# A three-stage attention and MLP kernel: a new order of the middle stage with eight exponential buffers, stack loads ahead in their block, whole-chunk loads for the attention output, and ten instead of twelve warming matmuls

## The chip, the cores and the metric

The kernel runs on one core of one Trainium2 chip. The metric is the device time of one execution in microseconds. Before the change it is 696.94 us, the median of three runs (695.82 to 697.39). A core has a matrix engine (PE, with its weight loads PEld), a vector engine (DVE), an activation engine (ACT), a general engine (POOL) and a queue engine (SP) that issues most of the DMAs here. Each engine works through its own list in order; between engines and DMAs stand semaphores.

## The reference

The output mixes two branches per token, with a gate from the token itself:

```python
x = A_x                                                  # 1 x 2048 x 512
g = sigmoid((x * gate_w).sum(-1, keepdims=True))
qkv = x @ wqkv                                           # 32 heads of 16
scores = einsum("bhqd,bhkd->bhqk", q, k) * 16 ** -0.5
mask = (i - j >= 0) & (i - j < 256)                      # sliding causal window
a = (softmax(where(mask, scores, -1e9)) @ v) @ wo
y = (x - mean(x)) / sqrt(var(x) + 1e-5)
b = gelu(y @ w1 + b1) @ w2 + b2                          # 512 -> 1792 -> 512
out = g * a + (1 - g) * b
```

Everything is float32. The kernel splits each operand of a large matmul into a high and a low part and adds three products (high x high, low x high, high x low), so a 512-deep product takes twelve matmuls of 128 x 128 x 512.

## The kernel before

The program has three stages, and its tile framework is told not to reorder: the instructions of each engine stand in the order in which the Python code emits them.

**Stage 1** (to 145 us in the profile) projects x to q, k and v. It opens with `first_units`: a zeroed tile `idle` is multiplied with itself twelve times (L265) while the first weights and the first chunk of x arrive, then 24 matmuls (L281) make the first two q/k units. q and k go to DRAM in a layout from which "stacks" of four heads are loaded later.

**Stage 2** (145.3 to 494.5 us) interleaves attention and the first MLP layer on PE. The table `ORDER` is a string of 1202 letters, and `run` emits one piece of work for each:

- `S` (`s_pair`, L348): scores of one block of 128 queries, for the row maximum alone; read by DVE (L357, L358).
- `T` (`st_pair`, L403): the transposed scores of one block of keys, with the maximum in two extra rows; ACT exponentiates them (L405) and POOL zeroes what the mask forbids (L407). There are eight groups `p` of four heads, sixteen blocks `kb` each, and two `T` (pr 0 and 1) per block.
- `P` (`pv`, L422): 32 matmuls that multiply the exponentials of up to four key blocks with v, for two blocks of queries; ACT copies the result out.
- `f` (`fill`, L626): one step, two matmuls, of a unit of the first MLP layer; 24 steps make a unit, of which there are 28. ACT copies the unit's two halves to `t` tiles (`out_half`), and SP stores them to `hp`.

All four take their PSUM from four buffers of two banks, `ring`: the next piece takes the buffer that was used longest ago, and a unit of the MLP keeps one for its 24 steps. The exponentials of a key block live in one of seven slots taken in rotation (`p_tile`), three and two in two tiles and two in the spare `x8` tiles `extra`. There are nine `t` tiles, which hold the halves, raw weights and the collected outputs of `P` (`acc`).

At the start of each block `kb`, `block` first calls `tick()`, which emits what earlier pieces left for later (stores of `hp` and `osc`, weight swaps), and then, for even `kb`, the two DMAs of `load_stacks` (L335), which bring 256 columns of the next group's q and k; the `S` of the next group run about six blocks ahead of its `T`. The maxima go out and come back as DMAs (`md`, L376 and L382).

**Stage 3** (from 494.5 us) runs the second MLP layer in 56 steps of twelve matmuls (`mlp2`, L834; four chunks of 512 tokens with 14 steps each). Into each chunk go four attention output units of twelve matmuls (`attn_out`, L813), one per 128 tokens. In `attn_out(c)`, SP loads the softmax sums (`su`, L785), DVE inverts them two steps later (`inv`, L790), SP stores the inverse (`rd`, L791), and then for each 128 tokens `loads(b)` issues eight DMAs, four of the attention output `osc` (L797) and four of the repeated inverse (L798), 64 KB each, into two `t` tiles. `scale` (L801) multiplies them two steps after that, ACT and DVE split the product, and one step later come the matmuls. Stage 3 has 44 `t` tiles.

## Time and profile before

| what | value |
|---|---|
| median of three runs | 696.94 us (695.82 to 697.39) |
| the profiled execution | 699.85 us, of which 698.0 us from its first to its last instruction (the span) |
| granted TensorE clock, mean | 0.999 |
| busy: PE, PEld | 688.7 us (99%), 536.0 us (77%) |
| busy: DVE, ACT, POOL | 474.9 us (68%), 385.1 us (55%), 268.8 us (39%) |
| DMA | 137.93 MB, mean 198 GB/s |

A row of the profile names the source line, the engine, the operation and the tiles it writes and reads (out<-in), then the shape and the count; behind a bar stand busy time, mean duration and idle time. A row of the timeline gives the start, the length of a run of equal instructions, and in brackets the engine's idle time before it with what ended it. A matmul's record begins when it begins to stream and ends when its result is out, so the records of neighbours overlap, and the distance between two starts tells the pace, not the length of one. A small wait between two matmuls therefore does not show as idle time of PE.

### The profile page before, as it was taken

What the parts mean: (1) busy time and instruction counts of PE and PEld (TensorE: products, weight loads), DVE (VectorE), ACT (ScalarE), POOL (GpSimd) and SP (SyncE); (2) the same over time, 40 slices, a digit from 0 to 9 for tenths busy, and PEclk for the clock granted to TensorE, in tenths of its full rate; (3) what the DMA queues carried; (4) which work ended last, traced back from release to release, by engine and by line L of the source; (5) the groups of instructions that cost most, each with busy time, mean ns of one, the idle gap of its engine ahead of it and who ended that gap; (6) DMA issues with size and microseconds to landing.
All of it is one profiled execution on the core that took longest, in us unless ns stands there. A gap on an engine that the chain in (4) does not pass through costs nothing.

```text
span 698.0 us, 16035 instructions
## 1 busy us (share of the span) xinstructions
PE 688.7 (99%) x5740; PEld 536.0 (77%) x5740; DVE 474.9 (68%) x971; ACT 385.1 (55%) x639; POOL 268.8 (39%) x623
## 2 busy tenths in 40 slices
PE   9999999999999999999999999999999999999997
PEld 6887777877777767777787777777777788888886
DVE  6546779966868777777687786776456835645554
ACT  6447463457686775777767768677624414123121
POOL 6900156436476564755656656559000000000000
PEclk9999999999999999999999999999999999999999
DMA  8998888786565758647776656525856443543531
GB/s 311 363 319 259 251 253 261 231 258 192 181 217 171 218 171 262 187 147 231 204 218 190 200 163 186 165 92 191 282 167 186 146 142 116 169 139 111 183 108 60
DMA packets 102678, 137.93 MB, mean 198 GB/s; under 512 B 13928, under 2 KB 53800, under 8 KB 102472
## 3 DMA queue, kind: packets, MB, share of 16 engines
q1 hardware_dynamic: 97848, 128.66, 58.7%
q10 hardware_dynamic: 4752, 8.26, 3.6%
q8 instruction: 46, 0.75, 0.4%
q14 instruction: 32, 0.26, 0.1%
HBM read 81.53 MB, written 54.30 MB: 195 GB/s over the span
## 4 chain that ended last, share of the span: by engine, by line
PE 89%; SPq 3%; DMA 3%; DVE 1%; issue 1%; ACT 1%; POOL 1%; DVEq 0%; ACTq 0%
PE ps_b L626 21%; PE ps_a L834 17%; PE ps_d L294 12%; PE ps_b L422 12%; PE ps_b L403 7%; PE ps_b L348 7%; PE ps_d L324 6%; PE ps_o L813 5%; SPq L797 1%; SPq L798 1%; DMA b2s<-in_b 1%; PE ps_d L281 1%; PE ps_x L265 1%; DMA osc<-t 1%; PE ps_x L348 1%
## 5 line engine op out<-in xcount | busy, mean ns | idle before, releaser
L626 PE MATMUL ps_b<-x,w 64*128 64x512 f32 x1344 | 212.7, 396 | 0.3 <-ACT p L405 0.2
L407 POOL TENSOR_SCALAR_AFFINE_SELECT p<-p 128x256 f32<-128x256 f32 x344 | 133.3, 415 | 102.5 <-ACT p L405 99.6
L405 ACT ACTIVATE p<-ps_b 128x768 f32<-128x768 f32 (+2 forms) x184 | 137.9, 770 | 42.5 <-PE ps_b L403 32.1
L834 PE MATMUL ps_a<-x,t 128*128 128x512 f32 x648 | 150.6, 390 | 0.8 <-DVE t L686 0.8
L358 DVE TENSOR_REDUCE mx<-ps_b 128x2 f32<-128x512 f32 x208 | 144.1, 693 | 7.1
L834 PEld LDWEIGHTS ps_a<-x,t 128*128 128x128 f32 x648 | 121.4, 188 | 27.3 <-issue 1.2
L626 PEld LDWEIGHTS ps_b<-x,w 64*128 64x128 f32 x1344 | 129.2, 186 | 11.9 <-issue 2.9
L357 DVE COPY_PREDICATED ps_b<-tri,ps_b 128x256 f32<-128x256 uint8 x208 | 88.3, 425 | 50.1 <-PE ps_b L348 34.7
L403 PE MATMUL ps_b<-qk 50*128 50x384 f32 (+5 forms) x512 | 90.3, 344 | 0.5 <-DVE mx L358 0.3
L348 PE MATMUL ps_b<-qk 62*128 62x384 f32 (+3 forms) x472 | 85.2, 346 | 1.4 <-DMA qk<-qk 1.3
L294 PE MATMUL ps_d<-x,w 128*128 128x512 f32 x360 | 84.8, 391 | 0.0
L294 PEld LDWEIGHTS ps_d<-x,w 128*128 128x128 f32 x360 | 67.3, 188 | 14.5 <-issue 0.5
L422 PE MATMUL ps_b<-p,v 128*32 128x256 f32 (+1 forms) x1376 | 74.9, 329 | 0.4 <-POOL p L407 0.4
L122 ACT ACTIVATE t<-ps_b 128x512 f32<-128x512 f32 (+1 forms) x112 | 52.0, 490 | 40.0 <-PE ps_b L422 32.8
L403 PEld LDWEIGHTS ps_b<-qk 64*128 64x128 f32 (+1 forms) x512 | 50.9, 184 | 20.7 <-issue 6.5
L407 POOL TENSOR_SCALAR_AFFINE_SELECT x<-x 128x256 f32<-128x256 f32 x136 | 52.2, 410 | 35.4 <-ACT x L405 35.1
L405 ACT ACTIVATE x<-ps_b 128x768 f32<-128x768 f32 (+2 forms) x72 | 55.0, 778 | 16.4 <-PE ps_b L403 13.6
L348 PEld LDWEIGHTS ps_b<-qk 62*128 62x128 f32 (+1 forms) x472 | 46.3, 184 | 17.9 <-ACT p L405 4.0
L422 PEld LDWEIGHTS ps_b<-p,v 128*32 128x32 f32 x1376 | 39.1, 110 | 26.5 <-ACT p L405 3.5
L119 DVE TENSOR_TENSOR t<-t,t 128x512 fp32r<-128x512 f32 x70 | 48.5, 692 | 14.6 <-ACT t L122 10.9
L122 ACT ACTIVATE t<-t 128x512 fp32r<-128x512 f32 x16 | 10.1, 632 | 81.7 <-DVE t L801 37.0
L682 ACT ACTIVATE t<-t,b1s 128x512 f32<-128x512 f32 x56 | 37.8, 715 | 25.4 <-DMA t<-hp 24.9
(87 smaller groups left out, 672.4 us busy)
## 6 DMA issues: line engine op xcount, KB each, us to landing
qk<-qk SPq DMA_DIRECT2D x112, 196.0 KB
t<-hp SPq DMA_DIRECT2D x56, 256.0 KB
hp<-t SPq DMA_DIRECT2D x52, 256.0 KB
qk<-t SPq DMA_DIRECT2D x48, 256.0 KB
osc<-t SPq DMA_DIRECT2D x31, 256.0 KB
t<-in_w SPq DMA_DIRECT2D x28, 256.0 KB
w<-w SPq DMA_DIRECT2D x28, 256.0 KB
qk<-t ACTq DMA_DIRECT2D x24, 256.0 KB
```

The source lines that it names most:

```text
L119: eng.tensor_tensor(out=lo, in0=src, in1=f32(hi), op=ALU.subtract)
L122: act.activation(dst, src, AF.Copy)
L294: pe.matmul(o, a[:, dt * 128:(dt + 1) * 128], b[:, dt * C:(dt + 1) * C], start=n == 0, stop=n == 11)
L348: pe.matmul(o[:, e, :n], qs[pr][r:k, qb * 128:qb * 128 + 128], ks[pr][r:k, t0:t0 + n], start=True, stop=True)
L357: dve.copy_predicated(o[:, :, :128], tri, o[:, :, 256:384])
L358: dve.tensor_reduce(m, o[:, :, :256], mybir.AxisListType.X, ALU.max)
L403: pe.matmul(o[:, e, :w], ks[pr][r:k, kb * 128:kb * 128 + 128], qs[pr][r:k, kb * 128:kb * 128 + w], start=True, stop=True)
L405: act.activation(pt[:, :, :w], o[:, :, :w], AF.Exp, scale=0.25)
L407: pool.affine_select(out=pt[:, :, a:a + 128], in_=pt[:, :, a:a + 128], pattern=[[0, 2], [sgn, 128]], base=b, channel_multiplier=-sgn, comp ...
L422: pe.matmul(a[32 * h:32 * h + 32, at:at + w], vs[:, kb, v:v + 32], pts[p, kb][:, h, fr:fr + w], start=n == 0, stop=n == len(parts) - 1, sk ...
L626: pe.matmul(o[:, e], w[kt // 4][r:r + 64, k, m:m + 128], y[r:r + 64, a:a + C], start=n == 0, stop=n == 23)
L834: pe.matmul(accs[c][b], x[:, b * 128:(b + 1) * 128], w, start=f == 0 and n == 0, stop=f == FT - 1 and n == 2)
```

## The change

Five places change. The text of `ORDER` is new throughout (1204 letters), and so its rows say little; the first line of each stands in the diff.

```diff
-ORDER = ("TfSffSffffTSffffTSfffTfSffTfSfffTSfffSPTSTSffffTSfffTfSfPTSffSfffTSffTffTfSfTffffSTPSTSPSTfTfffTSfff"
+ORDER = ("TfSfSfffffTfSfffTSfffTfSfffTSfffTfSffSPTSffTfSfffTSfffSPSTfSfffTfSfTffTffTSffTfffTSPSSTPSTfTfffTSffT"
...
+PICK = ("0000000000000000001000000000000000000001000100100000000000000000100001000100000000000001000000000000"
...
-    ring = []
+    ring, picks = [], list(PICK)
+
+    def choose():
+        return ring.pop(int(picks.pop(0)) if picks else 0)
 
     def two():
         if not ring:
             return ps("x", (128, 2, 512))
-        ring.append(ring.pop(0))
+        ring.append(choose())
         return ps(ring[-1], (128, 2, 512))
...
-        dve.memset(idle, 0.0)
+        dve.memset(idle[:, :256], 0.0)
         idle = idle.bitcast(BF16)
         o = two()[:, 0]
-        for _ in range(12):
+        for _ in range(10):
             pe.matmul(o, idle[:, :128], idle[:, :512], start=True, stop=True)
...
         if j % 2 == 0:
-            acc[p] = t2()
+            sums.append(sums.pop(0))
+            acc[p] = sums[-1]
...
-    nt[0] = 9
+    nt[0] = 6
...
-    extra = [f32(x8())[:, :1536].rearrange("p (h n) -> p h n", h=4) for _ in range(2)]
+    extra = [f32(x8()) for _ in range(2)]
+    sums = [t[:, 1536:] for t in extra]
+    extra = [t[:, :1536].rearrange("p (h n) -> p h n", h=4) for t in extra]
...
-    slots = [get("work", "p3", 1, (128, 3, 4, 384)), get("work", "p2", 1, (128, 2, 4, 384))]
-    slots = [slots[0][:, 0], slots[0][:, 1], extra[0], slots[0][:, 2], slots[1][:, 0], extra[1], slots[1][:, 1]]
+    low, high = (get("work", t, 1, (128, 3, 4, 384)) for t in ("pa", "pb"))
+    slots = [low[:, 0], low[:, 1], extra[0], low[:, 2], high[:, 0], extra[1], high[:, 1], high[:, 2]]
 
     def p_tile():
         np_[0] += 1
-        return slots[(np_[0] - 1) % 7]
+        return slots[(np_[0] - 1) % 8]
...
     def mlp1_unit(f, cp):
-        held = ring.pop(0)
+        held = choose()
...
     def block(p, kb):
-        tick()
         if kb % 2 == 0:
             if kb and p + 1 < 8:
                 load_stacks(p + 1, kb * 128 - 256, 256)
             if not kb and p:
                 load_stacks(p, S - 256, 256)
+        tick()
...
-    nt[0] = 44
+    nt[0] = 36
...
+        o = get("work", "oa", 1, (128, 4, 512))
+
+        def load_o():
+            for g in range(NG):
+                sp.dma_start(o[:, g], view(osc, [32 * S, HG], [S, DH], [1, C], off=g * 256 * S + c * C))
+
+        if c:
+            load_o()
 
         def inv():
             dve.reciprocal(su, su)
             sp.dma_start(view(rd, [128, 128], [1, 128]), su)
             us[c] = get("work", "us", 2, (128, 4, 512))
-
-        def loads(b):
-            o, r = t2(F32, (128, 4, 128)), t2(F32, (128, 4, 128))
+            r = get("work", "ra", 1, (128, 4, 512))
+            if not c:
+                load_o()
             for g in range(NG):
-                sp.dma_start(o[:, g], view(osc, [32 * S, HG], [S, DH], [1, 128], off=g * 256 * S + c * C + b * 128))
-                sp.dma_start(r[:, g], view(rd, [C, HG], [0, DH], [1, 128], off=g * HG * C + b * 128))
-
-            def scale():
-                dve.tensor_tensor(out=o, in0=o, in1=r, op=ALU.mult)
-                h, l = t2(F32R, (128, 4, 128)), t2(F32R, (128, 4, 128))
-                copy(h, o)
-                lo_part(l, o, h)
-                after(1, lambda: mm(h, l))
...
+                sp.dma_start(r[:, g], view(rd, [C, HG], [0, DH], [1, C], off=g * HG * C))
+            for b in range(4):
+                after(3 + b, lambda b=b: scale(b, *(t[:, :, b * 128:b * 128 + 128] for t in (o, r))))
...
-            after(2, scale)
+            after(1, mm)
 
         after(2, inv)
-        for b in range(4):
-            after(3 + b, lambda b=b: loads(b))
```

`PICK` says for each piece which of the free PSUM buffers it takes (0 is the one used longest ago; 522 of its 583 entries are 0, 60 are 1, one is 2). The eighth exponential slot takes the memory of three `t` tiles, and the collected outputs of `P` move to the unused ends of the two `extra` tiles. In stage 3, `inv` now emits the loads of a whole chunk and asks for `scale(b)` three to six steps after itself, which is the step where it stood before, so that the order on PE there stays what it was; `oa` and `ra` take the memory of eight `t` tiles. Line numbers behind the first edits grow: L335 is now L344, L403 is L412, L422 is L431, L626 is L638, L797 is L804 and L798 is L817.

The change moves instructions at three places of which the prediction speaks. First SP's list in chunk 0 of stage 3, from the sums' loads on; `w` are raw weights, `hp` the stored first-layer halves. Before:

```order
L785 DMA su_7623<-osc 32x1x128 x4
L655 DMA t_7646<-in_w 128x512
L679 DMA t_7648<-hp 128x512
L791 DMA rd_7628<-su_7623 128x128
L655 DMA t_7670<-in_w 128x512
L679 DMA t_7672<-hp 128x512
L797 DMA t_7693<-osc 128x1x128
L798 DMA t_7694<-rd_7628 128x1x128
L797 DMA t_7693<-osc 128x1x128
L798 DMA t_7694<-rd_7628 128x1x128
```

and with the change:

```order
L797 DMA su_7589<-osc 32x1x128 x4
L667 DMA t_7613<-in_w 128x512
L691 DMA t_7615<-hp 128x512
L811 DMA rd_7594<-su_7589 128x128
L804 DMA oa_7595<-osc 128x1x512 x4
L817 DMA ra_7637<-rd_7594 128x1x512 x4
L667 DMA t_7646<-in_w 128x512
L691 DMA t_7648<-hp 128x512
L667 DMA t_7670<-in_w 128x512
L691 DMA t_7672<-hp 128x512
```

The four pairs for the first 128 tokens, and 24 more DMAs for the other three quarters behind them, become eight DMAs directly behind the store of the inverse, and the loads of step 11 stand behind these.

Second, SP's list in stage 2 around the stacks of group 3, columns 1024 to 1279 (`qk<-qk_1`, `qk<-qk_0`; the one of `qk_0_69` onto itself is a copy in DRAM). Before:

```order
L522 DMA w_3228<-w_3227 64x1024 x2
L639 DMA hp<-t_3441 128x512
L639 DMA hp<-t_3443 128x512
L435 DMA osc<-t_3470 128x512
L335 DMA qk_79<-qk_1_68 98x2x256
L335 DMA qk_79<-qk_0_67 98x2x256
L315 DMA qk_0_69<-qk_0_69 16x8x512
L376 DMA md_3452<-ms_3451 4x32x32
```

and with the change:

```order
L532 DMA w_3234<-w_3233 64x1024 x2
L651 DMA hp<-t_3430 128x512
L651 DMA hp<-t_3432 128x512
L344 DMA qk_79<-qk_1_68 98x2x256
L344 DMA qk_79<-qk_0_67 98x2x256
L445 DMA osc<-x_254_1522 128x512
L324 DMA qk_0_69<-qk_0_69 16x8x512
L385 DMA md_3441<-ms_3440 4x32x32
```

The stacks pass the store of `osc`.

Third, PE's list at the end of stage 2, around the last `P` but one (its four rows of matmuls into one PSUM tile). Before:

```order
L403 MATMUL ps_b_1122_7385<-qk_79 128x256 x2
L403 MATMUL ps_b_1123_7390<-qk_79 128x256 x2
L422 MATMUL ps_b_1124_7395<-p_256_1526,v_80 32x256 x4
L422 MATMUL ps_b_1124_7395<-p_255_1525,v_80 32x128 x4
L422 MATMUL ps_b_1124_7395<-x_254_1524,v_80 32x256 x4
L422 MATMUL ps_b_1124_7395<-p_256_1526,v_80 32x128 x4
L403 MATMUL ps_b_1126_7418<-qk_79 128x128 x2
L403 MATMUL ps_b_1127_7423<-qk_79 128x128 x2
```

and with the change:

```order
L412 MATMUL ps_b_1091_7352<-qk_79 128x256 x2
L412 MATMUL ps_b_1092_7357<-qk_79 128x256 x2
L638 MATMUL ps_b_1061_7140<-x_212_1256,w_5787 128x512 x2
L412 MATMUL ps_b_1095_7374<-qk_79 128x128 x2
L412 MATMUL ps_b_1096_7379<-qk_79 128x128 x2
L638 MATMUL ps_b_1097_7384<-x_193_1143,w_6234 128x512 x2
L431 MATMUL ps_b_1098_7387<-pa_1523,v_80 32x256 x4
L431 MATMUL ps_b_1098_7387<-x_253_1521,v_80 32x128 x4
L431 MATMUL ps_b_1098_7387<-pb_1524,v_80 32x256 x4
L431 MATMUL ps_b_1098_7387<-x_254_1522,v_80 32x128 x4
```

Two MLP steps and the last two `T` now stand ahead of this `P` instead of behind it.

36 lines of the change are left out of this document (23 added, 13 removed).

## The prediction

> **What bounds the kernel now.** I read the page first, then the waits of PE, then the busy time by stage.
>
> ```profile
> PE 688.7 (99%) x5740; PEld 536.0 (77%) x5740; DVE 474.9 (68%) x971; ACT 385.1 (55%) x639; POOL 268.8 (39%) x623
> PE ps_b L348 <- DMA qk<-qk: 1.3, 1, 1.3
> PE ps_a L834 <- DVE t L686: 0.8, 1, 0.8
> 145.30:494.50 349.20, 346.57 (x4249) 261.95 (x4248) 261.67 (x588) 250.45 (x384) 209.96 (x552) 1.00 0.62 193
> 494.50:545.30 50.80, 49.58 (x211) 38.64 (x210) 28.42 (x50) 21.98 (x37) 0.00 (x0) 1.00 0.60 188
> 545.30:694.00 148.70, 148.70 (x657) 122.90 (x655) 81.02 (x137) 39.68 (x62) 0.00 (x0) 1.00 0.41 131
> ```
>
> PE is busy for 99% of the span, and its waits view has two entries in stages 2 and 3 above 0.5 us. (The rows of stages give length, then PE, PEld, DVE, ACT, POOL, clock, DMA share, GB/s.) Read so, nothing but matmuls could be gained. But records of neighbours overlap, so the loss must be read from the distance between starts:
>
> ```profile
> 568.80 2.88 PE L813 MATMUL ps_o<-w,t 128*128 128x512 f32 x12
> 571.52 2.88 PE L834 MATMUL ps_a<-x,t 128*128 128x512 f32 x12
> 467.10 1.51 PE L422 MATMUL ps_b<-p,v 128*32 128x256 f32 x32
> 468.42 0.61 PE L422 MATMUL ps_b<-x,v 128*32 128x256 f32 x8
> 472.37 0.34 PE L403 MATMUL ps_b<-qk 64*128 64x384 f32 x2
> 472.55 0.40 PE L626 MATMUL ps_b<-x,w 64*128 64x512 f32 x2
> L626 PE MATMUL ps_b<-x,w 64*128 64x512 f32 x1344 | 212.7, 396 | 0.3 <-ACT p L405 0.2
> ```
>
> Twelve matmuls of 512 columns take 2.72 us at pace, 0.227 each; one `P` (32 records) 1.32; a full `T` or `S` up to 0.18 (472.37 to 472.55); an MLP step, two matmuls side by side, as long as one of 512 columns. Stage 2 holds 672 steps (1344 records), 256 `T` and 236 `S`, of which some are narrower, and 64 `P`, of which eight are half: 672 x 0.227 + 492 x 0.17 (less 5 for the narrow ones) + 60 x 1.32 = 152.5 + 78.6 + 79.2 = 310 us. It lasts 349.2. So some 39 us of stage 2 are lost in pieces too small for the waits view, and this is what a new order can win or lose. In stage 3 the same pace shows no loss from 545 us on (the groups from 568.80 stand 2.72 apart), and some in chunk 0.
>
> **The start: ten warming matmuls.**
>
> ```profile
> 0.98 0.48 DVE L261 MEMSET t<- 128x512 f32 x1 [0.98 <-PEq L874]
> 1.52 5.30 PE L265 MATMUL ps_x<-t 128*128 128x512 bf16 x12 [1.52 <-DVE t L261]
> 5.34 0.15 PEld L265 LDWEIGHTS <-t 128*128 128x128 bf16 x1 [0.28 <-issue]
> 5.76 0.15 PEld L265 LDWEIGHTS <-t 128*128 128x128 bf16 x1 [0.28 <-issue]
> 5.06 0.43 DVE L236 CAST x<-v 128x512 fp32r<-128x512 f32 x1 [3.59 <-DMA v<-in_xt]
> 5.23 0.51 ACT L122 ACTIVATE w<-wv 128x128 fp32r<-128x128 f32 x2 [1.73 <-DMA wv<-in_wq]
> 5.98 0.68 DVE L119 TENSOR_TENSOR x<-v,x 128x512 fp32r<-128x512 f32 x1
> 6.26 6.41 PE L281 MATMUL ps_d<-x,w 128*128 128x512 f32 x24
> 6.26:7.40 1.14, 1.14 (x2) 0.93 (x3) 1.00 1.05 404
> ```
>
> A warming matmul takes 0.427 us (their weight loads stand 0.42 to 0.43 apart), twice the later pace. The first real operands are there at 5.49 (x) and about 5.5 (w), but the last warming matmul starts at 6.19 and holds PE to 6.61; by 7.40 only two real matmuls have begun (the last row), also at 0.43. With ten, and with a memset of half the columns (0.24 us less), the warming ends at 1.28 + 10 x 0.427 = 5.55. PE has 1.06 us more for real matmuls. If the clock rises at the same moment, 2.5 of them run in that time at half speed, worth 2.5 x 0.227 = 0.57 us. The next operand, the low part of x, is there at 6.66 and needed at 5.55 + 4 x 0.427 = 7.26, so nothing new waits. Ends: 1.06 gained if the clock rises earlier by as much, nothing if it rises later by the same. I take **-0.55**, the row of the two slow real matmuls being the nearest.
>
> **Stage 2: stacks first.** The one visible wait is a DMA:
>
> ```profile
> 262.61 1.28 SPq L435 DMA_DIRECT2D osc<-t  x1
> 263.98 1.79 SPq L335 DMA_DIRECT2D qk<-qk  x2
> 269.61 0.44 PE L348 MATMUL ps_b<-qk 62*128 62x384 f32 x2 [1.32 <-DMA qk<-qk]
> ```
>
> SP held the store of `osc` for 1.28 us and only then issued the stacks, which the `S` at 269.61 waited for. With the stacks ahead of that store they go out up to 1.35 us earlier; in the new order this `S` also stands behind one more `T`. The wait goes: **-1.35**. Between none and all of it lie 0 and -1.5.
>
> **Stage 2: fewer turns to `P`.** Entering and leaving a `P` costs time:
>
> ```profile
> 474.44 0.64 PE L626 MATMUL ps_b<-x,w 64*128 64x512 f32 x4
> 475.01 0.64 PE L422 MATMUL ps_b<-x,v 128*32 128x256 f32 x8
> 476.45 0.50 PE L626 MATMUL ps_b<-x,w 64*128 64x512 f32 x2
> ```
>
> Two steps from 474.44 should end at 474.90 and `P` starts at 475.01; `P` should end at 476.33 and the next step starts at 476.45: 0.11 + 0.12. Two `P` in a row follow each other without loss (467.10 to 468.42). In the old table `P` stands in 62 places alone or in a run, in the new one in 57: 5 x 0.22 = **-1.1**.
>
> **Stage 2: its end.**
>
> ```profile
> 484.37 0.86 PE L422 MATMUL ps_b<-p,v 128*32 128x256 f32 x16
> 486.25 0.41 PE L422 MATMUL ps_b<-p,v 128*32 128x128 f32 x4 [0.38 <-POOL p L407]
> 486.59 0.44 PE L403 MATMUL ps_b<-qk 64*128 64x128 f32 x4
> ```
>
> This `P` lasted 2.22 instead of 1.44 (1.32 and its exit), 0.78 lost to POOL's last selects. The new order puts two steps and two narrow `T` ahead of it, 2 x 0.227 + 2 x 0.06 = 0.57 more for POOL: **-0.55**.
>
> **Stage 2: the rest of the order.** 39 less these is still some 36 us. Pieces that follow each other without a step between them (`ST`, `TS`, `TT`, `SS`) are 126 in the old table and 135 in the new; the buffer of an `S` is taken again within 1.2 us of PE work once in the old and never in the new, that of a `T` 29 and 35 times. I see no gain of size in such counts and take 0; but a new order has stalls of its own, and since those I struck off were two in 349 us worth 2.1, I charge one such, **+1.0**. Bounds: a tenth of 39 either way, -4 to +4. The eighth slot costs POOL and ACT nothing (same work); six `t` tiles instead of nine stand against two halves per unit of 12 us, so they turn over in about 30 us, longer than any store here: 0.
>
> **Stage 3, chunk 0.**
>
> ```profile
> 510.99 0.33 SPq L791 DMA_DIRECT2D rd<-su  x1
> 516.72 0.57 SPq L798 DMA_DIRECT2D t<-rd  x1
> 519.30 0.69 DVE L801 TENSOR_TENSOR t<-t,t 128x512 f32<-128x512 f32 x1 [3.40 <-DMA t<-rd]
> 520.71 3.06 PE L813 MATMUL ps_o<-w,t 128*128 128x512 f32 x12
> 541.18 5.12 PE L834 MATMUL ps_a<-x,t 128*128 128x512 f32 x20
> 7.40:12.51 5.11, 5.11 (x23) 3.94 (x21) 1.00 1.01 361
> DMA packets 102678, 137.93 MB, mean 198 GB/s; under 512 B 13928, under 2 KB 53800, under 8 KB 102472
> ```
>
> From 520.71 to 541.18 stand seven groups of twelve, 19.04 us at pace; they take 20.47. These 1.43 us are the four output units, each waiting a little for a product that DVE could only make when the last of eight loads had landed, SP issuing 32 of them at 0.6 us. With whole-chunk loads SP issues eight (4.8 us, from 511.3 to about 516.2), and quarters 1 to 3 find everything there: -1.1. For quarter 0 the last load is issued 1.1 us earlier (516.2 against 517.29) but moves 256 KB instead of 64 behind 1.8 MB: 2.1 MB at the 361 GB/s of the window at the start, where the DMA engines were full, are 5.8 us from about 512.8, so 518.6, and with completion about 519 against 519.3 before: about the same. The wait for `su` ahead of it (the 0.8 in the waits of PE) is untouched. A late unit also delays the steps behind it (0.4 us around 544): -0.1 of it. **-1.2**, bounds 0 and -1.8. In chunks 1 to 3 there is no loss to win, and PE's order stays.
>
> **Sum.** -0.55 - 1.35 - 1.1 - 0.55 + 1.0 - 1.2 = -3.75. The profiled execution took 699.85 (span 698.0), 2.9 above the median; the difference carries over: a span of 694.25, and a median of 696.94 - 3.75 = **693.2**. What a measurement tells from no change is about 0.2%, 1.4 us.
>
> **The rivals.**
> *The order gives nothing back* (0.17): its own stalls eat what the struck ones gave, so only start and stage 3 remain: -1.75, 695.2. For it: the counts above are level. Against: fewer turns to `P` is arithmetic.
> *The order gives more* (0.10): eight slots and `PICK` take another 3.3 of the 36 us: 689.9.
> *SP stands still* (0.11), the slower side. A stack load must wait until PE has read the columns that it overwrites:
>
> ```profile
> SPq L335 <- PE ps_b L403: 13.2, 16, 2.8
> SPq L382 <- DMA md<-ms: 52.6, 26, 4.0
> ```
>
> Put first, it waits for the `T` just emitted, up to 2.8 us, with the maxima (L376, L382), `hp` and `osc` behind it. `T` waits for the maxima. Each such stall costs about the 1.3 us seen at 269.61; five of some thirty groups make +6.5: -3.75 + 6.5 = +2.75, 699.7. It decides from three on. Against: from a group's last maximum load to its first `T` the table leaves at least 2.9 us of PE work, 7 on average.
> *The burst holds back quarter 0* (0.08): at the mean 198 GB/s of the span instead of 361 the loads land at 523.4, the first output unit starts at 524.8, 4.1 late: 693.2 + 4.1 = 697.3.
> *The clock rises later* (0.07): a us more in the slow stretch costs 1 - 0.227/0.427 = 0.47. The three runs spread 1.57 us; as much more makes 694.8. By the Trainium skill, "TensorE: Matmul & The Clock Gate" (Part 1: The HAM clock gate), the clock follows a free-running window of about 3.4 us that does not start with the kernel, so the moment would be independent of how many matmuls warm it and could fall up to a window later, 3.4 x 0.47 = 1.6 us by an estimate from that page. The trace agrees in so far as the clock rose 5.9 us after the first matmul, more than one window and less than two; one execution cannot show the spread.
>
> **How the numbers follow.** The forecast has 0.47; its own range is 691.0 to 695.4 (the order's term and stage 3's). The range 689.0 to 697.4 holds it and every rival but the third and the far side of the second, some 0.16 left out. Faster by over 0.2% (below 695.5): forecast 0.46, the second rival 0.10, of the first 0.10, of the clock's 0.06: 0.72. Slower (above 698.3): 0.11. The rest, 0.17, is no change.
>
> **What would show it.** Start: L281 begins its 24 at about 5.5 us, and the first matmul of L294 stands near 11.95 instead of 12.51. Stacks: no wait of PE on `qk<-qk`. Stage 2 lasts 347.2 us. Its last `P` but one lasts under 1.7. Chunk 0: the seven groups in 19.4. A stage 2 of over 350 us, waits of PE on `qk<-md`, or a first group of L813 more than 11 us behind the `rd` store (9.7 now) would make the prediction wrong.

## The result and the profile after

The changed kernel took 725.31 us (median of 4, 722.52 to 730.05), the kernel before on the same chip 697.16 (median of 4, 695.82 to 699.70): a ratio of 1.041, 95% interval 1.034 to 1.047. The forecast was 693.2, range 689.0 to 697.4. It is wrong in sign and by 32 us.

The profiled execution of the changed kernel took 725.02 us. Its page, with the busy time and the row of the granted clock over 40 slices of the span:

```profile
PE 690.4 (96%) x5738; PEld 543.8 (75%) x5738; DVE 475.0 (66%) x971; ACT 383.9 (53%) x639; POOL 267.7 (37%) x623
PEclk9999999999999999999999999999899899989999
```

PE's busy time hardly moved (688.7 before), its share fell from 99% to 96%, and three slices near the end show a lower clock. The stages, in the columns of the prediction's rows of stages (length, PE, PEld, DVE, ACT, POOL, clock, DMA share, GB/s), from the first `T` to the first step of the second MLP layer and from there to the end:

```profile
144.88:490.48 345.60, 342.37 (x4249) 265.09 (x4248) 260.90 (x588) 249.78 (x384) 210.48 (x552) 1.00 0.61 196
490.48:723.00 232.52, 205.28 (x866) 167.24 (x864) 109.52 (x187) 61.84 (x98) 0.00 (x0) 0.94 0.40 127
```

Stage 2 is 3.7 us shorter than before (144.88 to 490.48 against 145.24 to 494.54, 349.30). Stage 3 lasts 232.52 instead of 203.46 (494.54 to 698.00). So the whole loss is in stage 3, and it is 29 us there. PE's waits name the place:

```profile
PE ps_o L833 <- ACT t L131: 23.3, 4, 8.1
PE ps_b L412 <- DMA qk<-md: 1.7, 3, 0.8
```

L833 is the matmul of an attention output unit (L813 before); ACT's L131 copies the scaled quarter that it multiplies. It waits four times, once in each chunk, 23.3 us in all. The timeline of PE at those places (start, length, idle time ahead of it and what ended that):

```profile
523.40 4.44 PE L833 MATMUL ps_o<-w,t 128*128 128x512 f32 x12 [8.12 <-ACT t L131]
527.68 2.88 PE L852 MATMUL ps_a<-x,t 128*128 128x512 f32 x12
530.40 2.88 PE L833 MATMUL ps_o<-w,t 128*128 128x512 f32 x12
577.23 4.81 PE L833 MATMUL ps_o<-w,t 128*128 128x512 f32 x12 [5.52 <-ACT t L131]
633.19 5.49 PE L833 MATMUL ps_o<-w,t 128*128 128x512 f32 x12 [4.91 <-ACT t L131]
689.99 4.61 PE L833 MATMUL ps_o<-w,t 128*128 128x512 f32 x12 [4.75 <-ACT t L131]
```

The first unit of each chunk comes late; from the second unit on the groups stand 2.72 us apart without a wait. But the group behind a gap also takes longer, 4.28 us to the next one instead of 2.72. The clock says why:

```profile
523.40:526.60 3.20, 3.20 (x8) 2.56 (x9) 2.91 (x5) 1.24 (x3) 0.00 (x0) 0.51 0.98 357
526.60:530.00 3.40, 3.40 (x17) 2.81 (x16) 2.03 (x4) 2.29 (x4) 0.00 (x0) 1.00 0.28 108
```

The first 3.20 us hold only 8 matmuls, at a clock of 0.51, and the next 3.40 hold 17 at full clock. In the trace's clock records it stands at half from 519.7 to 526.5, 574.3 to 581.1, 632.3 to 639.2 and 690.4 to 693.8. Adding what each matmul there took beyond 0.227 us gives 1.6 + 1.9 + 2.9 + 1.7 = 8.1 us. Gaps and clock are 31.4 us.

What the first unit waits for is its scaled quarter, and DVE makes it at L822 when `oa` and `ra` have landed. DVE and SP in chunk 0:

```profile
521.95 0.69 DVE L822 TENSOR_TENSOR oa<-oa,ra 128x512 f32<-128x512 f32 x1 [13.08 <-DMA t<-in_w]
503.96 0.33 SPq L811 DMA_DIRECT2D rd<-su  x1
504.34 2.51 SPq L804 DMA_DIRECT2D oa<-osc  x4
506.95 3.25 SPq L817 DMA_DIRECT2D ra<-rd  x4
```

SP did what the prediction said: the eight loads are out by 510.2, earlier than I had put it. They landed only by 521.9. (The releaser that the DVE row names, a load of `in_w`, is the one that came last by the profile; the operands are `oa` and `ra`.) From 507 to 511 almost nothing else was moving; the packets of that stretch, and their queue's share of 16 DMA engines:

```profile
DMA packets 301, 0.59 MB, mean 148 GB/s; under 512 B 18, under 2 KB 18, under 8 KB 300
q1 hardware_dynamic: 300, 0.58, 47.0%
```

Every one of these loads had more queued behind it, and still less than half of the engines' time was used: 47% of 16 engines is about 8 packets in flight at any time, not 16. 2.1 MB at 148 GB/s are 14.2 us.

### The profile page after: what moved, and what is told of

Read it like the earlier page. It is cut to its first block, busy times and chain, and to the rows that moved or that the text cites. A ratio compares the mean times of both kernels' runs of the same rounds, so it can differ in the third digit from the quotient of the medians.

```text
span 723.0 us, 15772 instructions
## 1 busy us (share of the span) xinstructions
PE 690.4 (96%) x5738; PEld 543.8 (75%) x5738; DVE 475.0 (66%) x971; ACT 383.9 (53%) x639; POOL 267.7 (37%) x623
## 4 chain that ended last, share of the span: by engine, by line
PE 66%; DMA 19%; DVE 5%; SPq 4%; ACT 3%; issue 2%; ACTq 0%; POOL 0%; DVEq 0%
PE ps_b L638 20%; PE ps_b L431 11%; PE ps_a L852 10%; PE ps_o L833 7%; PE ps_b L412 6%; PE ps_b L357 6%; PE ps_d L303 4%; DMA t<-hp 4%; DMA rd<-su 3%; PE ps_d L333 2%; DMA qk<-qk 2%; DMA md<-ms 2%; DMA qk<-md 1%; DMA su<-osc 1%; ACT t L131 1%
## 5 line engine op out<-in xcount | busy, mean ns | idle before, releaser
L638 PE MATMUL ps_b<-x,w 64*128 64x512 f32 x1344 | 211.1, 395 | 0.2 <-ACT pb L414 0.2
L638 PEld LDWEIGHTS ps_b<-x,w 64*128 64x128 f32 x1344 | 130.2, 186 | 10.6 <-issue 2.0
L416 POOL TENSOR_SCALAR_AFFINE_SELECT pa<-pa 128x256 f32<-128x256 f32 x192 | 74.3, 414 | 68.5 <-ACT pa L414 67.9
L412 PE MATMUL ps_b<-qk 64*128 64x384 f32 (+5 forms) x512 | 89.0, 337 | 2.2 <-DMA qk<-md 1.7
L414 ACT ACTIVATE pa<-ps_b 128x768 f32<-128x768 f32 x96 | 76.6, 813 | 26.2 <-PE ps_b L412 18.2
L303 PE MATMUL ps_d<-x,w 128*128 128x512 f32 x360 | 84.8, 391 | 0.0
L357 PE MATMUL ps_b<-qk 62*128 62x384 f32 (+2 forms) x472 | 83.0, 343 | 0.2
L303 PEld LDWEIGHTS ps_d<-x,w 128*128 128x128 f32 x360 | 67.3, 188 | 14.6 <-issue 0.5
L416 POOL TENSOR_SCALAR_AFFINE_SELECT pb<-pb 128x256 f32<-128x256 f32 x160 | 62.6, 419 | 39.0 <-ACT pb L414 38.3
L833 PE MATMUL ps_o<-w,t 128*128 128x512 f32 x192 | 53.9, 437 | 23.3 <-ACT t L131 23.3
L414 ACT ACTIVATE pb<-ps_b 128x768 f32<-128x768 f32 (+2 forms) x96 | 65.5, 706 | 17.5 <-PE ps_b L412 13.8
L833 PEld LDWEIGHTS ps_o<-w,t 128*128 128x128 f32 x192 | 40.9, 215 | 34.1 <-ACT t L131 25.0
L412 PEld LDWEIGHTS ps_b<-qk 50*128 50x128 f32 (+1 forms) x512 | 50.9, 184 | 18.7 <-issue 5.0
L131 ACT ACTIVATE t<-oa 128x512 fp32r<-128x512 f32 x16 | 10.1, 631 | 100.5 <-DVE oa L822 63.0
L414 ACT ACTIVATE x<-ps_b 128x768 f32<-128x768 f32 x64 | 51.1, 813 | 14.5 <-PE ps_b L412 12.4
```

Of the source, the lines that this page charges most:

```text
L303: pe.matmul(o, a[:, dt * 128:(dt + 1) * 128], b[:, dt * C:(dt + 1) * C], start=n == 0, stop=n == 11)
L357: pe.matmul(o[:, e, :n], qs[pr][r:k, qb * 128:qb * 128 + 128], ks[pr][r:k, t0:t0 + n], start=True, stop=True)
L412: pe.matmul(o[:, e, :w], ks[pr][r:k, kb * 128:kb * 128 + 128], qs[pr][r:k, kb * 128:kb * 128 + w], start=True, stop=True)
L414: act.activation(pt[:, :, :w], o[:, :, :w], AF.Exp, scale=0.25)
L416: pool.affine_select(out=pt[:, :, a:a + 128], in_=pt[:, :, a:a + 128], pattern=[[0, 2], [sgn, 128]], base=b, channel_multiplier=-sgn, comp ...
L638: pe.matmul(o[:, e], w[kt // 4][r:r + 64, k, m:m + 128], y[r:r + 64, a:a + C], start=n == 0, stop=n == 23)
```

## The experiments

The theories at the outset: **(1)** a load is spread over no more DMA engines than the slowest dimension of its access pattern allows, here the 8 heads of a group, and so half of the engines set the time; **(2)** reading each row of `rd` sixteen times, or the memory, is slow; **(3)** 36 `t` tiles are too few and hold SP; **(4)** in chunks 1 to 3 the store of `rd` is queued behind `oa`; **(5)** the clock's drop costs by itself. Times are medians; each ratio is to the kernel before on the same chip, with its 95% interval. Before lay at 697.2 to 699.7 from one set of runs to the next, so ratios are what is compared where the sets differ.

| run | us | ratio | stage 2 | stage 3 |
|---|---|---|---|---|
| changed kernel | 725.31 | 1.041 (1.034 to 1.047) | 345.60 | 232.52 |
| quarter loads | 693.53 | 0.9927 (0.9907 to 0.9948) | 344.71 | 200.61 |
| chunk loads only | 728.49 | 1.0435 (1.0396 to 1.0474) | 349.53 | 232.10 |
| sixteen first | 696.81 | 0.9967 (0.9942 to 0.9993) | 345.00 | 202.98 |
| store first | 722.78 | 1.0352 (1.0317 to 1.0387) | 345.08 | 233.15 |
| sixteen, step later | 692.58 | 0.9898 (0.9877 to 0.9919) | 344.39 | 200.87 |
| step later | 713.96 | 1.0186 (1.0152 to 1.0220) | 344.62 | 220.16 |
| stacks behind | 694.14 | 0.9923 (0.9903 to 0.9943) | 347.52 | 201.06 |
| no `PICK` | 701.62 | 1.0038 (1.0024 to 1.0053) | 353.08 | 200.85 |
| twelve warm | 693.57 | 0.9928 (0.9913 to 0.9944) | 346.29 | 200.90 |
| four first | 766.05 | 1.0962 (1.0926 to 1.0999) | 344.89 | 275.33 |
| old order, sixteen | 698.75 | 1.0008 (0.9992 to 1.0024) | 350.38 | 200.87 |
| before again | 698.81 | 1.0017 (0.9993 to 1.0040) | 349.10 | 201.60 |

The stages are those of each run's profiled execution.

### Quarter loads

```diff
-    nt[0] = 36
+    nt[0] = 44
-            r = get("work", "ra", 1, (128, 4, 512))
-            ...
+        def loads(b):
+            o, r = t2(F32, (128, 4, 128)), t2(F32, (128, 4, 128))
+            ...
```

> The changed kernel with the attention output's loads of before (eight of 128 columns per quarter, 44 `t` tiles); all else as changed. If the whole loss is in the chunk-wide loads (every theory that puts the cause there): stage 3 lasts 203.5 us as before, the 3.3 us of stage 2 and about 0.5 us of the start stay, so 697.2 - 3.8 = 693.4. If instead the new order of stage 2 leaves something late that stage 3 pays for: still above 710, with PE idle ahead of the first output unit.

693.53, within 0.2 us of the time expected, but that time was reckoned from 697.2 and before took 699.14 in this set: the gain is 5.6 us and not 3.8, since stage 3 came out at 200.61 and not 203.5. The stages of its profile (2 and 3):

```profile
145.88:490.59 344.71, 342.28 (x4250) 263.98 (x4249) 260.83 (x588) 249.51 (x384) 209.83 (x552) 1.00 0.62 196
490.59:691.20 200.61, 196.66 (x866) 161.92 (x864) 110.38 (x187) 61.55 (x98) 0.00 (x0) 1.00 0.47 150
```

With the loads of before, stage 3 keeps none of the loss: all else in the change together is worth 0.7% (0.5 to 0.9), and the chunk-wide loads are the whole of what went wrong. They also are not what stage 3 needed: with the new order, quarter loads leave it at 200.61.

### Chunk loads only

```diff
 (the kernel before)
-    nt[0] = 44
+    nt[0] = 36
+        o = get("work", "oa", 1, (128, 4, 512))
+        ...  attn_out as in the change
```

> The kernel before with only the chunk-wide loads of the change (36 `t` tiles, `oa` and `ra`). If they alone lose: stage 3 lasts about 232 us as in the changed kernel, 697.2 + 29 = 726, with the four gaps of 5 to 8 us. If the loss needs the new order too: under 710.

728.49, 29.4 more than before, with four gaps of PE that sum to 22.7 us; its row of stage 3:

```profile
494.90:727.00 232.10, 205.51 (x866) 167.47 (x864) 109.58 (x188) 61.87 (x98) 0.00 (x0) 0.95 0.39 129
```

The loads lose as much with the old order. Both ways around, it is this one part.

### Sixteen first

```diff
-  view(osc, [32 * S, HG], [S, DH], [1, C], off=g * 256 * S + c * C)
+  view(osc, [S, DH], [32 * S, HG], [1, C], off=g * 256 * S + c * C)
-  view(rd, [C, HG], [0, DH], [1, C], off=g * HG * C)
+  view(rd, [0, DH], [C, HG], [1, C], off=g * HG * C)
-  sp.dma_start(raw, wo[dt])
+  sp.dma_start(raw, view(wo, [D, DH], [DH * D, HG], [1, D], off=dt * 128 * D))
```

> The changed kernel with the rows of `oa`, `ra` and of `wo` in the order (element of a head, head) instead of (head, element): the slowest dimension of each chunk-wide load is then 16 instead of 8; bytes, packets, number of loads and order of issue stay. Theory 1 (a load is spread over as many DMA engines as its slowest dimension allows, 8 of 16): about 16 packets of `oa` and `ra` in flight instead of 8, the 2.1 MB take some 6.7 us instead of 13.3, no gap ahead of the first output unit of chunk 0 nor of the others, no drop of the clock, stage 3 at 202 to 204 us, 691 to 694. Theory 2 (the repeated read of each row of `rd`, or the memory itself, is slow): the loads take as long as now, the gaps stay, 725. Theory 3 (36 `t` tiles are too few and hold SP back): also 725.

The gaps are gone but for two, 1.9 us in all. The packets from 505.5 to 508, while `oa` and `ra` load, and then, from the timeline, the first unit of chunk 0:

```profile
DMA packets 413, 0.77 MB, mean 308 GB/s; under 512 B 44, under 2 KB 44, under 8 KB 412
q1 hardware_dynamic: 412, 0.75, 94.4%
```

```profile
515.97 2.37 PE L833 MATMUL ps_o<-w,t 128*128 128x512 f32 x9 [1.55 <-ACT t L131]
```

Same bytes, same packets of 2048 bytes, same number of loads, the same sixteen reads of each row of `rd`, the same 36 `t` tiles: only the order of the rows differs, and the rate doubled, from 148 to 308 GB/s, with 94% of the engines' time used instead of 47%. Theory 1 stands, 2 and 3 fall. The Trainium skill, "DMA: Bandwidth & Descriptors" (Why a DMA increments its semaphore by 16 and not by 1), states this rule: the number of engines is the largest one up to 16 that divides the slowest dimension, not counting those of size 1, on both sides. The traces agree: 8 heads, 47%; 16 elements, 94%. Its time, 696.81, is 3 us more than I expected, with executions from 693.87 to 698.91; the profiled one (694.54) is among the shorter. Its first units have next to nothing to spare (1.55 us late in chunk 0, 0.35 in chunk 3).

### Store first

```diff
-        if c:
-            load_o()
...
-            if not c:
-                load_o()
+            load_o()
```

> The changed kernel with `oa` loaded behind the store of `rd` in every chunk, as it is in chunk 0 (in chunks 1 to 3 it went ahead of it). Chunk 0 is untouched: its gap of 8 us and the slow clock behind it stay. In chunks 1 to 3 theory 4 (the store of `rd` stands 6.5 us behind the packets of `oa`, and `ra` behind the store) gives `ra` back about 5 us: gaps of 5.5, 4.9 and 4.8 us fall to 0 to 1, and with them the drop of the clock (1.7 to 3.0 us each), 725.3 - 20 = 705. If the two loads share the same eight engines and only their sum of 13.3 us counts: data from about 557.5 to 571, due at 570.3, gaps of 1 to 2.5 us without a drop, about 709 to 712. If the order does nothing: 725.

722.78 (1.0352; the interval overlaps that of the changed kernel), far from 705 or 710. First the changed kernel's SP in chunk 1, then this run's SP and PE there:

```profile
558.97 0.33 SPq L811 DMA_DIRECT2D rd<-su  x1
565.57 2.47 SPq L817 DMA_DIRECT2D ra<-rd  x4
```

```profile
559.30 0.33 SPq L808 DMA_DIRECT2D rd<-su  x1
559.72 2.51 SPq L804 DMA_DIRECT2D oa<-osc  x4
562.28 2.46 SPq L813 DMA_DIRECT2D ra<-rd  x4
579.16 4.50 PE L829 MATMUL ps_o<-w,t 128*128 128x512 f32 x12 [6.22 <-ACT t L131]
```

In the changed kernel `ra` went out 6.6 us behind the store, whose packets stood behind those of `oa`. Here it goes out 3.3 us earlier, and the first unit is no earlier (6.22 late against 5.52). The order of the two does not matter, so theory 4 is not the cause. Of the expectations the last, no gain, is the nearest; the two with a gain missed. I had the eight engines free for these loads, but from 567 on loads of `hp` are in flight with them: 16 packets in flight instead of 8, and the median packet of 2048 bytes takes some 150 ns (568 to 571 us) instead of 84 (562 to 565 us). That the `hp` loads hold back the others on the same engines is read from this and was not tried.

### Sixteen first, a step later

```diff
 (sixteen first)
-                after(3 + b, lambda b=b: scale(...))
+                after(4 + b, lambda b=b: scale(...))
```

> The run with sixteen first, and in it the four scalings one MLP step (2.72 us of PE) later, so that the loads have that much more time. In the run with sixteen first alone the first output unit of chunk 0 still waited 1.55 us for its scaled quarter, that of chunk 3 0.35 us, with nothing to spare in chunks 1 and 2 either. If that small lead is what is left over: no wait of PE on `ps_o`, the clock full throughout stage 3, 690 to 692 and less spread from run to run. If the move costs elsewhere (the products stand one step closer to the chunk's last accumulation): 694 or more, and waits at L852 or L859.

692.58, a ratio of 0.9898: the fastest of all, 1% below the kernel before and, by the ratios, 4.9% below the changed one. Stage 3, and the units of chunk 0 at even distance:

```profile
489.83:690.70 200.87, 196.73 (x866) 161.99 (x864) 109.10 (x187) 62.42 (x98) 0.00 (x0) 1.00 0.44 147
```

```profile
517.18 2.88 PE L833 MATMUL ps_o<-w,t 128*128 128x512 f32 x12
519.90 2.88 PE L852 MATMUL ps_a<-x,t 128*128 128x512 f32 x12
522.62 2.88 PE L833 MATMUL ps_o<-w,t 128*128 128x512 f32 x12
```

No wait of PE on `ps_o` is left. Against quarter loads (0.9927) its interval overlaps: what chunk-wide loads bring over quarters, once they use all engines and have time, is too small to tell.

### A step later alone

```diff
 (the changed kernel)
-                after(3 + b, lambda b=b: scale(...))
+                after(4 + b, lambda b=b: scale(...))
```

> The changed kernel, loads of eight engines as they are, with the four scalings one MLP step later alone. Each gap of PE shrinks by 2.72 us: 8.1, 5.5, 4.9, 4.8 become 5.4, 2.8, 2.2, 2.0, which is 10.9 us. If the drop of the clock behind a gap costs by itself and needs a gap longer than about 3.4 us (theory 5): it stays in chunk 0 and is gone in chunks 1 to 3, another 1.9 + 3.0 + 1.7 = 6.6 us, so 725.3 - 17.5 = 707.8. If the clock drops behind the short gaps too: about 714. If the halved clock in the records cost nothing: 714 as well, but with the first groups behind the gaps at 2.72 us.

713.96. The gaps are 4.97, 3.20, 2.63 and 2.60 us, 13.4 in all. The second and third of them, each with the group that follows:

```profile
579.48 5.49 PE L833 MATMUL ps_o<-w,t 128*128 128x512 f32 x12 [3.20 <-ACT t L131]
584.76 3.34 PE L852 MATMUL ps_a<-x,t 128*128 128x512 f32 x12
634.25 3.04 PE L833 MATMUL ps_o<-w,t 128*128 128x512 f32 x12 [2.63 <-ACT t L131]
637.12 2.88 PE L852 MATMUL ps_a<-x,t 128*128 128x512 f32 x12
```

Behind 3.20 us the clock is halved and the group takes 5.28 us; behind 2.63 and 2.60 it is full and the group takes 2.87. So the drop is a cost of its own (theory 5). But the length of the gap is not what decides. Behind the 3.20 us the clock fell at 578.81, only 2.54 us into the gap; and in the same profile a gap of 1.88 us in stage 1 (98.50 to 100.38) was followed by half clock too, from 100.95 to 107.78.

In each of the fourteen traces the clock changes only at whole multiples of 3.413 us from its first rise (in the changed kernel, 4.28 and 519.70 are 151 of them apart). So its time runs in periods of that length. Five periods of this profile (length, PE's busy time, clock, DMA share, GB/s):

```profile
97.54:100.95 3.41, 1.40 (x7) 1.00 0.79 240
575.40:578.81 3.41, 0.87 (x4) 1.00 1.05 304
578.81:582.22 3.41, 2.75 (x7) 0.50 0.96 367
630.01:633.42 3.41, 1.61 (x8) 1.00 1.04 279
633.42:636.84 3.42, 2.59 (x11) 1.00 0.97 369
```

The first two periods, with 1.40 and 0.87 us of busy PE, are followed by half clock (the first has the gap of 1.88 us and 0.13 of other idle time). The third gap lies across two periods, which keep 1.61 and 2.59 us of work, and the clock stays full. In all fourteen traces a period at full clock with 1.40 us of work or less was followed by half clock, and one with 1.54 or more was not: 2.0 us of idle PE within one period halved the clock, and 1.9 did not. The Trainium skill, "TensorE: Matmul & The Clock Gate" (Part 1: The HAM clock gate), has the clock halve after an idle window of about 3.4 us; the traces agree with it on the length of the period, but not on how much of it must be idle: 2.0 us were enough here.

The expectation's condition, a gap longer than about 3.4 us, thus failed. The time is that of the branch in which the clock drops behind the short gaps too, 714, but for other reasons: the gaps shrank by 9.9 instead of 10.9, and only the first two lost their clock. The profiled execution (716.70, the longest of its four) also began stage 2 at 150.02, some 5 us later than the others, after the gap and the slow clock in stage 1. Stage 3 alone is 12.4 us shorter than the changed kernel's: 9.9 of gaps, and the rest, some 2.5, about what the clock gave back (4.9 us of slow matmuls instead of 8.1).

### Stacks behind

```diff
 (sixteen first, a step later)
     def block(p, kb):
+        tick()
         if kb % 2 == 0:
             ...
-        tick()
```

> The run before last in this list (sixteen first, a step later) with one part of the change undone: the loads of the stacks go out behind the due work of their block again, as in the kernel before. If the term of the prediction is right (the stacks ahead of the `osc` store take away the one wait on `qk<-qk`): that wait of 1.3 us is back and the time is 1.0 to 1.5 us longer than that run's. If the new order hides it anyway: no difference, no wait on `qk<-qk` above 0.5. If stacks first cost SP (the rival of the prediction): shorter than that run's.

694.14 (0.9923 against 0.9898, and the intervals overlap). Stage 2 is 347.52 instead of 344.39, and in the waits of PE the one on the stacks is there, three times (sum, count, longest):

```profile
PE ps_b L357 <- DMA qk<-qk: 2.5, 3, 1.4
```

Stacks first is worth 3.1 us of stage 2 in these two profiles and 1.6 by the medians. But the seven other profiles with stacks first and `PICK` have a stage 2 of 344.62 to 346.29, so the 3.1 could be as little as 1.2; and stacks first does not always remove the wait: it is 0.8 us in the run with quarter loads and 1.4 in the one with twelve warming matmuls. The term's cause is seen; its size is not settled.

### No `PICK`

```diff
 (sixteen first, a step later)
-PICK = ("0000...")
+PICK = ""
```

> Sixteen first, a step later, with the table `PICK` left empty, so that the PSUM tags go around in turn as in the kernel before. The prediction gave `PICK` no term of its own. If it is worth nothing: stage 2 lasts 345.9 us as in the changed kernel and the time is that of the run with it, within 0.7. If it is what brought the 1.3 us of stage 2 beyond the prediction: stage 2 at 347.2 or more.

701.62, 9.0 more than with the table. Its row of stage 2, and the first of its waits of PE:

```profile
144.87:497.95 353.08, 347.72 (x4249) 268.54 (x4248) 261.93 (x588) 250.13 (x384) 210.18 (x552) 1.00 0.60 192
```

```profile
PE ps_b L352 <- DVE mx L362: 1.3, 4, 0.4
```

This is the surprise of the study: the choice of which PSUM tag comes next, to which the prediction gave no term, is worth 8.7 us in these two profiles, and 6.8 against the longest stage 2 of the others (346.29). Without it the new order is slower than the old one, 353.08 against 349.3. (The prediction named `PICK` once, in its second rival, with the eighth slot, at 3.3 us and a chance of 0.10.) The loss accrues evenly (2.2 us after 800 matmuls of stage 2, 4.1 after 1600, 7.1 after 3200, 8.7 at the end) in pieces of 0.5 us and less. Waits for DVE's reading of the maxima are the largest that the waits show, 3.3 us in three rows; where the rest lies is not shown.

### Twelve warming matmuls

```diff
 (sixteen first, a step later)
-        dve.memset(idle[:, :256], 0.0)
+        dve.memset(idle, 0.0)
-        for _ in range(10):
+        for _ in range(12):
```

> The best run so far (sixteen first, scalings a step later) with the start of the kernel before: twelve warming matmuls and the memset of 512 columns. If the term of the prediction is right: the first matmul of L303 about 0.55 us later than with ten (11.54 in that run), 12.1, and the time longer by as much, 693.1, which is below what the measurement can tell. If what counts is only when the clock rises: 11.4 to 12.5, whichever way the moment falls, and no difference.

693.57 (0.9928; 0.9898 with ten, the intervals just overlap). L290 begins at 6.26 and L303 at

```profile
12.18 2.20 PE L303 MATMUL ps_d<-x,w 128*128 128x512 f32 x9
```

in its timeline, against 5.58 and 11.54 with ten. Over the profiles at hand the first matmul of L303 (L294) stands at 12.51, 12.18, 12.04, 11.75 and 11.44 with twelve, mean 11.98, and at 11.49 to 11.89 with ten, mean 11.67 of nine. Two fewer are worth 0.3 us on average. With twelve the spread is a microsecond and follows the moment at which the clock rises (7.46, 6.82, 6.48, 5.89 and 5.18 us, in the same order); with ten that moment lies between 4.28 and 7.11, and the spread is only 0.4. In this run stage 2 was 1.9 us longer too, which the start does not explain, so the difference of the medians is not its measure.

### Four first

```diff
 (the changed kernel)
-  sp.dma_start(o[:, g], view(osc, [32 * S, HG], [S, DH], [1, C], ...))
+  for q in range(2):
+      sp.dma_start(o[64 * q:64 * q + 64, g], view(osc, [32 * S, 4], [S, DH], [1, C], ...))
 (and `ra` likewise)
```

> The changed kernel with each chunk-wide load of `oa` and `ra` in two halves of 64 rows, so that the slowest dimension of each is 4 (sixteen loads a chunk, the same 2048-byte packets). Theory 1 (as many engines as that dimension, and always the same ones): 4 packets of them in flight where nothing else loads, about 75 GB/s, 2.1 MB in about 27 us instead of 13.3, each gap some 13 us longer, 725 + 4 x 13 = 777 or more. If a load's engines follow on from the last one's, two halves share out over 8: about 725 as now. If the engines had nothing to do with it: 725, or some 2 us per chunk more for eight more issues.

766.05. The packets from 510 to 520, while only these loads are in flight, and the first gap:

```profile
DMA packets 505, 0.97 MB, mean 97 GB/s; under 512 B 31, under 2 KB 31, under 8 KB 505
q1 hardware_dynamic: 505, 0.97, 26.2%
```

```profile
533.58 5.49 PE L836 MATMUL ps_o<-w,t 128*128 128x512 f32 x12 [17.52 <-ACT t L131]
```

A quarter of the engines' time with a slowest dimension of 4, and two halves of a load do not spread over eight: they share the same four. The same section of the Trainium skill says so too (a load takes the lowest-numbered engines); the rate shows that both halves share their engines, and no run here shows which ones. The gaps are 17.5, 16.1, 16.1 and 14.7 us, 41 more than in the changed kernel; I expected 13 each and it was 10: an engine moved 24 GB/s here (97 by 4) and 18.5 in the changed kernel (148 by 8).

### Old order, sixteen first

```diff
 (chunk loads only, and in it)
+  sixteen first, a step later
```

> The kernel before (old order, seven slots, twelve warming matmuls, stacks behind) with chunk-wide loads alone, rows in the order (element, head) and scalings a step later. If the prediction's term for chunk 0 holds once the loads are quick: 699.4 - 1.2 = 698.2, stage 3 at 202.3 us or less instead of 203.5. If all of stage 3's loss goes with it: stage 3 at 200.9, 696.8. If the old order's end leaves stage 3 late anyway: 699.4.

698.75, a ratio of 1.0008: nothing that can be measured, though its stage 3 lasted 200.87 us against 203.46 in the first profile of before. Stage 3 of that profile, and then of this run:

```profile
494.54:698.00 203.46, 198.33 (x866) 161.53 (x864) 110.40 (x188) 61.66 (x98) 0.00 (x0) 1.00 0.46 147
```

```profile
495.23:696.10 200.87, 196.72 (x866) 162.00 (x864) 109.28 (x188) 62.47 (x98) 0.00 (x0) 1.00 0.44 149
```

### Before again

No edit.

> The kernel before, unchanged, profiled once more, to see whether the 1.4 us that its four output units of chunk 0 lost in the first profile (stage 3 at 203.5 us) are a property of its quarter loads. If they are: stage 3 at about 203.5 again, and chunk-wide loads with sixteen first (stage 3 at 200.9 with the old order) should have gained 2.6 us in time, which their runs did not show. If they belonged to that one execution, which took 2.9 us more than the median of its kernel: stage 3 near 200.9 with no loss ahead of L813, and the prediction's term for chunk 0 had nothing to win.

Its profiled execution took 698.8 us (span 696.9), nearer to the median of its kernel. Its row of stage 3, and from its timeline the first output unit of chunk 0 and the step behind the last:

```profile
495.30:696.90 201.60, 197.51 (x866) 161.61 (x864) 110.31 (x188) 61.76 (x98) 0.00 (x0) 1.00 0.46 147
```

```profile
519.93 2.94 PE L813 MATMUL ps_o<-w,t 128*128 128x512 f32 x12
540.11 5.12 PE L834 MATMUL ps_a<-x,t 128*128 128x512 f32 x20
```

Between the two: from 519.93 to 540.11 the seven groups take 20.18 us, 1.14 over pace, so the loss at the quarters is there again; but stage 3 is 1.9 us shorter than in the first profile, whose 0.97 at 511.98 and 0.24 ahead of the first unit are missing, and the wait on `qk<-qk` at L348 is 0.3 instead of 1.3. Between the two expectations, then: about 1.1 us belongs to the quarter loads, the rest to one execution.

## Why the prediction was wrong, point by point

**Stage 3, chunk 0: the step that failed.** The prediction took "2.1 MB at the 361 GB/s of the window at the start, where the DMA engines were full", and had the last load land at about 519. The rate of other loads was carried over to these. The loads of the start have 128 rows as their slowest dimension, these have 8, and they moved at 148 GB/s on half of the engines (308 with sixteen first, 97 with four). A row of before hints at it: with the same 8-head pattern, from 515.3 to 518,

```profile
DMA packets 709, 0.34 MB, mean 126 GB/s; under 512 B 44, under 2 KB 709, under 8 KB 709
q1 hardware_dynamic: 709, 0.34, 42.4%
```

the queue did not use half of the engines there either. It did not matter then, because each quarter needed only 0.5 MB before its unit could start. It is a warning rather than a proof, since SP's issuing (64 KB in 0.6 us, 109 GB/s) held those loads back too. The change made the first unit of a chunk wait for four times as much. In chunk 0 the loads had from about 506 to 513.8 (the unit was due at 523.40 - 8.12 = 515.28 and stands 1.45 behind its scaling), some 8 us, and took 16, of which their own bytes at 148 GB/s are 14.

**"In chunks 1 to 3 there is no loss to win, and PE's order stays."** True, and beside the point: there was a loss to make. I costed the edit only where a wait existed, not where it put 2.1 MB ahead of a unit that had had 0.5. Three of the four gaps, 15.2 of the 23.3 us, are in those chunks.

**The clock.** Not in the prediction for stage 3 at all: 8.1 of the 31.4 us lost come from half clock behind the four gaps of 4.75 to 8.12 us, each of which left PE idle for over 2.0 us of one of the clock's periods of 3.41 (see "A step later alone").

**The rival "the burst holds back quarter 0"** was the right mechanism: loads at about half the rate, first unit late. It was sized 4.1 us for one chunk by the mean rate of the span, 198 GB/s; the rate was 148, the delay 8.1, it came in all four chunks, and the clock came on top. Its mark held as well: the first group of L833 stood 19.4 us behind the `rd` store, where over 11 was named as the sign of a wrong prediction.

**Chunk 0's gain, -1.2.** Nothing measurable. Chunk loads that use all engines and have time, on the old order, give 1.0008 (0.9992 to 1.0024). Of the 1.43 us that I read off, 1.1 is in the second profile of before; the stage's other excess was that execution's own. With the new order quarter loads lose nothing (200.61).

**The start, -0.55.** Right in kind: 11.55 in the profile after (predicted 11.95, 12.51 before). By the profiles of all runs it is 0.3 on average. "So nothing new waits" did not hold: in the profile after, the weight loads of L290 wait 0.35 us at 6.66 for the split of x. The rival that the clock rises later had its price right: over the five profiles with twelve, 2.28 us of later rise go with 1.07 of delay, 0.47 a microsecond.

**Stacks first, -1.35.** Right cause, size open: 1.2 to 3.1 us of stage 2 with the new order, 1.6 by medians whose intervals overlap; and the wait on `qk<-qk` that was to be gone is there in two of the profiles with stacks first (0.8 and 1.4). The rival that SP stands still did not come: the waits on `qk<-md` sum to 1.7 us in the profile after, 0.8 at most, and two profiles of the old order have 0.9 and 1.1.

**Turns to `P`, -1.1.** Right: what is lost on entering and leaving `P`, over the records of all its turns, is 16.0 us in the first profile of before (126 changes) and 14.6 in the run with sixteen first and a step later (116 changes), -1.4.

**The end of stage 2, -0.55.** Wrong sign. The 0.9 at 486.59 is gone, but two narrow `T` and the `P` behind them now wait for ACT, 0.50 + 0.43 + 0.75 at 480 to 482: +0.8.

**The order's own stall, +1.0, and no term for `PICK`.** Both far off, and they cancel. `PICK` is worth -8.7. If this and the 1.2 to 3.1 of the stacks add up, the order without either would have a stage 2 of 354 to 356 us, some 5 to 7 above the old one. The new text of `ORDER` and the eighth slot were not tried apart, so what each does is open. Only the sum was near, and by luck: stage 2 came out 3.7 us shorter, -2.0 was predicted. I had counted the places where a PSUM buffer is taken again soon, and saw "no gain of size"; the gain was in the choice of the buffer itself, which no row of before could price. The bounds of a tenth of the 39 us were too narrow for it.

**The range.** The forecast's own range, 691.0 to 695.4, is narrower than the bounds that it names: -4 to +4 for the order's term and 0 to -1.8 for stage 3's give 687.6 to 697.4.

So the prediction without the chunk-wide loads (693.2 + 1.2 = 694.4, 2.5 us below before) has the right sign and under half the size of what that kernel gains, 5.6 us, partly by errors that cancel; and the one term that I took to be safely between 0 and -1.8 was worth about +30.

## What to carry to other kernels

Before joining small loads into large ones, look at the slowest dimension of each side's access pattern and at the share of the DMA engines that such loads reached so far; put a dimension of 16 outermost, as here, even at the price of permuting a weight's rows. Then count what must land before the first consumer starts, in every repetition of the stage, not only where the profile has a wait. A gap of PE can be paid twice: in these runs 2.0 us of idle within one of the clock's periods of 3.41 us halved it for one period or more, 1.6 to 2.9 us of extra time in the changed kernel, while a gap of 2.6 that lay across two periods cost no more than itself.

## What the runs showed of the hardware that was not expected

- The engines that a load uses follow its slowest dimension: 4, 8 and 16 gave 26%, 47% and 94% of the engines' time and 97, 148 and 308 GB/s with the same 2048-byte packets, and two loads of 4 in flight together did not reach 8.
- The TensorE clock changed only at whole multiples of 3.413 us from its first rise, in all fourteen traces. A period between two of them with 1.40 us of busy PE or less was followed by half clock, one with 1.54 or more was not; so a gap of 1.88 us (2.01 of idle in its period) was followed by half clock, and gaps of 2.60 and 2.63, each across two periods, were not.
- Two executions of one kernel differ by single waits of a microsecond (`qk<-qk` 1.3 and 0.3; stage 3 of before 203.46 and 201.60): a term read from one such wait has that uncertainty.
